# Softmax attention in phases of thirteen and twelve scores instead of sixteen

## The chip, the cores and the metric

The kernel runs on one core of a Trainium2 chip. The core has a matrix engine (TensorE, PE in the profile; PEld is its weight load), three engines for elementwise work (VectorE or DVE, ScalarE or ACT, GpSimd or POOL) and a queue that issues most of the DMA transfers (SP). TensorE writes to PSUM, a memory of eight banks of 512 float32 columns on 128 partitions. The metric is the device time of one execution in microseconds, the median of several.

## What is computed

Two blocks over the same 2048 tokens of 512 channels, mixed by a gate; all in float32.

```python
def _A_ref(x, wqkv, wo):
    H = 32; Dh = D // H                      # 32 heads of 16 channels
    q, k, v = qkv[0], qkv[1], qkv[2]
    scores = jnp.einsum("bhqd,bhkd->bhqk", q, k) * Dh ** -0.5
    p = _softmax(scores, axis=-1)
    o = jnp.einsum("bhqk,bhkd->bhqd", p, v)
    return o.transpose(0, 2, 1, 3).reshape(B, S, D) @ wo
def _B_ref(x, w1, b1, w2, b2):
    h = _layernorm(x, axis=-1)
    u = _gelu(jnp.einsum("bsd,sf->bdf", h, w1) + b1)      # F = 1792
    y = jnp.einsum("bdf,fs->bds", u, w2) + b2
    return y.transpose(0, 2, 1)
g = _sigmoid((x * gate_w).sum(-1, keepdims=True))
return g * _A_ref(x, A_wqkv, A_wo) + (1 - g) * _B_ref(x, ...)
```

The attention needs 32 x 2048 x 2048 exponentials, and only ScalarE computes them.

## The kernel before

The first 300 us project x to v, k and q and compute the first layer of block B. Then comes the attention, which fills the rest. The second layer of block B, and after it the output projection, are laid beside it on TensorE.

**Groups, scores and phases.** A group is two heads times half of the queries; there are 32 (`NG`). A *score* is one matmul of 128 keys by 512 queries for one head, into one PSUM bank, from a stack of K rows (`ks`) and one of Q rows (`qs`) that SP loads a group ahead (`load_q` at the group's first phase, `load_k` at its second; 8 and 6 DMAs). A group has 2 heads x 16 key blocks x 2 query blocks = 64 scores. They are worked off in four *phases* of sixteen (`PHASES, NSC = 4, 16`), 128 phases in all. The order of every engine's instructions in this part is the order of the code (`tc.manual_schedule`).

**One phase.** TensorE computes sixteen scores on half of its rows each; beside each of the first `n_b` of them, on the other half, runs a half of a matmul of the dense work (`dn`, up to 14 in a phase; a fence of a one-element memset on POOL, `token`, separates the two halves of the rows). The scores reach their exponentials in three ways. Four (`EVAC`) are copied out by DVE into `pe`, and ScalarE exponentiates the four in one instruction at the phase's end. Six (`SINGLE`) are read from PSUM one by one. Six form three doubles (`TWO`), each in two adjacent banks, exponentiated by one instruction of 1024 columns. Seven of the eight banks serve the scores; scores 7, 8 and 9 reuse banks of the first ones, and the doubles reuse banks of the others (`shares` gives which). After the scores follow the products with v: for each score two matmuls of 32 columns, added up in one bank (`av`), which DVE adds to the group's sum `ot`. The copied scores enter the products a phase later (`HELD`), and where it evens out, the last double too. After its last products a group's sum is stored by SP (`store`, eight DMAs), in the first phase of the next group, where the products run into two banks.

**Where the lines are.** L907 is the score matmul (tiles named `s`, or `t` for doubles), L916 the dense half beside it, L924 the copy by DVE, L928 a single exponential, L869 a double, L872 a double split into two singles (in a group's first phase, where one pair of banks must come free separately), L939 the block of four, L792 the products with v, L814 and L816 DVE's addition to the sum. L831 are dense matmuls that run before the loop. L492 fills constant rows of the K stacks. `later` holds work that DVE does after a phase's copies: splitting weights, inverting sums, and, at the change from second layer to output projection (`open_end`), constants for the end.

Of the kernel before, what the change touches and what calls it, by code (L numbers as in the profile page):

```python
# [16 lines left out]
SYNC = mybir.DependencyInfo(mybir.DependencyClass.Sync, mybir.DependencyReason.DATA)  # L17
REASON = "the two halves of the rows add to one bank"
# [40 lines left out]
def gated_mix(ctx: ExitStack, tc: tile.TileContext, a_x, a_wqkv, a_wo, b_w1, b_b1, b_w2, b_b2, gate_w, out):  # L59
# [438 lines left out]

    def stack(dst, src, which, pair, cols, planes):
        b, r0 = divmod(pair * 2 * DH, P)  # L500
        for i in range(2):
            rows = slice(r0 + i * DH, r0 + (i + 1) * DH)
            for row, *part in planes:
                at = slice(i * HALF + row, i * HALF + row + DH)
                nc.sync.dma_start(dst[at].bitcast(F32), src[b][part[which], rows, cols])
# [22 lines left out]
    PHASES, NSC, BANKS = 4, 16, 7  # L528
    LAST = NG * PHASES - 1
# [51 lines left out]
    def open_end():  # L581
# [6 lines left out]
        sums_of = end.tile([P, P], F32, name="sums_of")  # L588
        nc.vector.tensor_copy(
# [3 lines left out]
        least.append(end.tile([P, 1], F32, name="least"))  # L593
# [122 lines left out]
    for k in range(ND):  # L716
        call(6 * k + 5, load_wo, k, 6 * k + 5)
    steps = second_layer(0)
    first, at = steps[:28], put(steps[28:], 0, [14])
    for t in range(1, NS):  # L720
        at = put(second_layer(t), at, [14] * 3)
    for half in range(2):
        for k in range(ND):
            pairs = 3 if half and k == ND - 1 else 4
            p0 = PHASES * (half * NP + 4 * k + pairs) + 1
# [10 lines left out]
    p1 = PHASES * (NP + 2 * 4) + 3  # L736
    call(p1, fetch_o, 1, 0, (8, 9), (p1 + 2, p1 + 3, p1 + 3))
    call(p1 + 4, fetch_o, 1, 1, (10, 11), (p1 + 6, p1 + 7, p1 + 7))
    p2 = PHASES * (NP + 3 * 4) + 2
    assert p2 > 2 * at  # L740
    call(p2, fetch_o, 1, 2, (0, 1), (p2 + 1, p2 + 1, p2 + 1))
    call(p2 + 4, load_wq, p2 + 4)
    call(LAST - 1, fetch_o, 1, 3, (2, 3), (LAST, LAST, LAST), 3)
    for t in range(NH, NS):
        at = put_output(t, 6 if 2 * at < p2 + 2 else 8, at)
    assert at == NG * PHASES // 2
# [3 lines left out]
    EVAC = 1, 3, 5, 7  # L750
    SINGLE = 0, 2, 4, 6, 8, 9
    TWO = (10, 11), (12, 13), (14, 15)
    TURNS = [(0, 2), (4, 6), (8, 9), *TWO]
    HELD = [(1, 3), (5, 7)]

    def shares(n):

        for one in range(0, BANKS, 2):
            lows = [k for k in range(one)][::2] + [k for k in range(one + 1, BANKS)][::2]
            for third in lows:  # L760
                if n in (third, third + 1):
                    first, second = (low for low in lows if low != third)
                    return [first, first + 1, one, second, second + 1, 2 * third + 1 - n, n]

# [20 lines left out]
    def apply_v(av, grp, pairs, final=False):  # L785

        for n, pair in enumerate(pairs):
            for i, c, qb, pt in sorted(pair, key=lambda u: u[2]):
                for h in range(2):
                    j = 2 * qb + h  # L790
                    v_at = (c * H + grp % NP * 2 + i) * VC
                    nc.tensor.matmul(  # L792
                        av[32 * j : 32 * (j + 1), i * QC : (i + 1) * QC],
                        v_flat[:, v_at : v_at + 32],
                        pt[:, h * QC : (h + 1) * QC],
                        start=n == 0,
                        stop=n == len(pairs) - 1,
                    )
        covered = [{qb for pair in pairs for i, _, qb, _ in pair if i == n} for n in range(2)]
        assert all(len(c) != 1 for c in covered)  # L800
        if grp not in sums:
            sums[grp] = ot_pool.tile([P, NB], F32, name="ot"), [False, False]
        ot, begun = sums[grp]
        halves = [n for n in range(2) if covered[n]]
        if grp == NG - 1 and final:
            parts = [(x, y, True) for x, y in zip(column_halves(ot), column_halves(av))]
        elif len(halves) == 2 and begun[0] == begun[1]:
            parts = [(ot, av, begun[0])]
        else:
            cols = [slice(n * QC, (n + 1) * QC) for n in range(2)]  # L810
            parts = [(ot[:, cols[n]], av[:, cols[n]], begun[n]) for n in halves]
        for x, y, more in parts:
            if more:
                nc.vector.tensor_tensor(x, y, x, ALU.add)  # L814
            else:
                nc.vector.tensor_copy(x, y)  # L816
        for n in halves:
            begun[n] = True
        if final and grp < NG - 1:
            store(grp, sums.pop(grp)[0])  # L820

    engines = {getattr(mybir.EngineType, name) for name in ("PE", "Activation", "DVE", "Pool", "SP")}
    with tc.manual_schedule(engines=engines):
        kt, qt = {0: load_k(0)}, {0: load_q(0)}
        held, fence, turn, spare = [], None, 0, 0
# [9 lines left out]
        for p in range(LAST + 1):  # L835
            grp, ph = divmod(p, PHASES)
            second = ph % 2
            for what, *args in calls.get(p, ()):
                what(*args)
            if ph == 0:  # L840
                at = [[0, 0], [0, 0]]
                if grp + 1 < NG:
                    qt[grp + 1] = load_q(grp + 1)
            if ph == 1 and grp + 1 < NG:
                kt[grp + 1] = load_k(grp + 1)
# [3 lines left out]
            half = slice(0, HALF) if second else slice(HALF, P)  # L849

            head = [second if n < n_b else (n - n_b) % 2 for n in range(NSC)]
            qbs = {}
            for a, b in TURNS + HELD:
                if head[a] == head[b]:
                    qbs[a], qbs[b] = 0, 1
                else:
                    zero, one = (a, b) if head[a] == 0 else (b, a)
                    qbs[zero], qbs[one] = turn, 1 - turn
                    turn = 1 - turn

            swap = ph == PHASES - 1 and p < LAST and head[TWO[1][0]] == head[TWO[1][1]]
            order = [*TURNS[:4], TURNS[5], TURNS[4]] if swap else TURNS

            def exps(n):
                pt = ptp.tile([P, 2, NB], F32, name="p2", bufs=len(TWO) + 1)
                where = [share[(j - BANKS) % BANKS] for j in (n - 1, n)]
                low = min(where)
                if (low, low + 1) in twos:
                    nc.scalar.activation(pt, twos[low, low + 1], AF.Exp, scale=SCALE)  # L869
                else:  # L870
                    for m in range(2):
                        nc.scalar.activation(pt[:, m, :], twos[low + m], AF.Exp, scale=SCALE)  # L872
                for j, k in zip((n - 1, n), where):
                    units[j] = *units[j][:3], pt[:, k - low, :]

            evac = evp.tile([P, len(EVAC), NB], F32, name="pe")
            units = {}
            share = shares(spare)
            pool = regions()
            psum = pool.__enter__()  # L880
            ones = [psum.tile([P, NB], F32, name=f"s{n}") for n in range(BANKS)]
            for n in range(NSC):
                i, qb = head[n], qbs[n]
                c = at[i][qb]
                at[i][qb] += 1
                if n < TWO[0][0]:
                    if n >= BANKS:
                        ones[share[n - BANKS]] = psum.tile([P, NB], F32, name=f"s{share[n - BANKS]}")
                    s = ones[share[n % BANKS]]
                else:  # L890
                    if n == TWO[0][0]:
# [4 lines left out]
                        for low in range(BANKS):  # L896
                            if low == share[2]:
                                av = psum.tile([P, NB], F32, name="av")
                            elif low in share[3:5] and ph == 0:
                                twos[low] = psum.tile([P, NB], F32, name=f"s{low}")  # L900
                            elif low not in twos:
                                two = psum.tile([P, 2, NB], F32, name=f"t{low}")
                                twos[low], twos[low + 1] = two[:, 0, :], two[:, 1, :]
                                twos[low, low + 1] = two
                    s = twos[share[(n - BANKS) % BANKS]]
# [16 lines left out]
                if n in EVAC:  # L922
                    pt = evac[:, EVAC.index(n), :]
                    nc.vector.tensor_copy(pt, s)  # L924
                    units[n] = i, c, qb, pt
                elif n in SINGLE:
                    pt = ptp.tile([P, NB], F32, name="p1", bufs=len(SINGLE))
                    nc.scalar.activation(pt, s, AF.Exp, scale=SCALE)  # L928
                    units[n] = i, c, qb, pt
                else:  # L930
                    units[n] = i, c, qb, None
                    if n == TWO[0][1] or n == TWO[1][1] and not swap:
                        exps(n)
                    elif n == TWO[2][1]:
                        exps(n)
                        if swap:
                            exps(TWO[1][1])
# [202 lines left out]
```

## Time and profile before

| | us |
|---|---|
| median of 3 runs | 1293.9 (1292.6 to 1295.09) |
| the profiled execution | 1295.3 |
| its span in the trace | 1293.3 |
| attention: first score to the last phase's products | 304.7 to some 1272 |
| granted TensorE clock | 0.997 of full speed |

A row of the trace in order of time gives start, duration, engine, line, operation, output<-input, shape and the number of merged instructions; in a row of several, the duration reaches from the first start to the last end. The rows of stretches give, after the stretch and its length, busy time and instruction count of PE, PEld, DVE, ACT and POOL, then the clock, the DMA share and GB/s. Rows of the chain of waits give start, duration and what the chain ran through.

### The profile page before, as it was taken

The numbers are of one execution on the slowest core, as the hardware profiler recorded it, in microseconds if no ns is written. First come the engines' busy times: TensorE is split into PE (matmuls) and PEld (weight loads), VectorE is DVE, ScalarE is ACT, GpSimd is POOL, SyncE is SP. The second block draws the span as 40 slices with busy tenths as digits, with TensorE's granted clock in tenths as the row PEclk, the third lists the DMA queues.
The fourth block names the chain that finished last, engine by engine and source line by source line (L and its number), as shares of the span: only waits on it lengthen the run. The fifth ranks groups of instructions, "written<-read, shape, count | busy, mean of one in ns | idle before, by whom it ended". The sixth has DMA issues, their size and how long they took to land.

```text
span 1293.3 us, 33067 instructions
## 1 busy us (share of the span) xinstructions
PE 1280.4 (99%) x13278; PEld 850.4 (66%) x13278; DVE 671.0 (52%) x1155; ACT 1091.3 (84%) x1537; POOL 180.0 (14%) x272
## 2 busy tenths in 40 slices
PE   9999999999999999999999999999999999999997
PEld 7888888886666666666666666666665565655555
DVE  5675362438445545544544444454454665645555
ACT  3443343447999999999999999999999999999994
POOL 0210244553110111011011101101110000000000
PEclk9999999999999999999999999999999999999999
DMA  4497643327343343333334443333333654335411
GB/s 131 139 317 276 222 121 98 98 78 159 67 88 75 68 97 83 77 68 81 77 60 98 83 77 66 81 75 60 88 68 75 151 135 114 81 84 108 80 44 72
DMA packets 93581, 133.20 MB, mean 103 GB/s; under 512 B 16277, under 2 KB 55339, under 8 KB 90348
## 3 DMA queue, kind: packets, MB, share of 16 engines
q1 hardware_dynamic: 92844, 129.94, 41.2%
q8 instruction: 108, 1.77, 0.6%
q10 hardware_dynamic: 576, 1.05, 0.2%
q14 instruction: 53, 0.43, 0.1%
HBM read 97.00 MB, written 33.93 MB: 101 GB/s over the span
## 4 chain that ended last, share of the span: by engine, by line
PE 93%; ACT 4%; DVE 1%; issue 1%; DVEq 0%; ACTq 0%
PE av L792 28%; PE s L907 19%; PE acc L416 12%; PE t L907 10%; PE acc L73 10%; PE dn L916 6%; PE s L792 5%; ACT p L928 1%; ACT p L869 1%; ACT pe L939 1%; PE pa L996 1%; DVE pe L924 1%; PE acc L187 1%; PE dn L831 1%; PE acc L254 0%
## 5 line engine op out<-in xcount | busy, mean ns | idle before, releaser
L928 ACT ACTIVATE p<-s 128x512 f32<-128x512 f32 x768 | 395.7, 648 | 6.1 <-PE s L907 3.6
L869 ACT ACTIVATE p<-t 128x1024 f32<-128x1024 f32 x352 | 348.4, 1131 | 0.0
L907 PE MATMUL s<-qs,ks 64*128 64x512 f32 x1344 | 343.0, 404 | 1.1 <-DVE pe L924 0.7
L924 DVE COPY pe<-s 128x512 f32<-128x512 f32 x512 | 317.8, 683 | 6.9 <-PE s L907 6.4
L907 PEld LDWEIGHTS s<-qs,ks 64*128 64x128 f32 x1344 | 232.9, 184 | 97.5 <-issue 52.4
L792 PE MATMUL av<-p,v 128*32 128x256 f32 x4872 | 285.4, 379 | 0.0
L814 DVE TENSOR_TENSOR ot<-av,ot 128x512 f32<-128x512 f32 (+1 forms) x128 | 73.5, 575 | 396.6 <-PE av L792 396.6
L939 ACT ACTIVATE pe<-pe 128x2048 f32<-128x2048 f32 x129 | 259.5, 2014 | 0.0
L792 PEld LDWEIGHTS av<-p,v 128*32 128x32 f32 x4872 | 158.4, 110 | 104.9 <-issue 0.7
L907 PE MATMUL t<-qs,ks 64*128 64x512 f32 x704 | 185.1, 445 | 2.9 <-ACT p L928 0.4
L916 PE MATMUL dn<-u_lo,w_hi 64*128 64x512 f32 x430 | 174.1, 405 | 0.0
L916 PE MATMUL dn<-u_hi,w_lo 64*128 64x512 f32 x430 | 173.9, 404 | 0.0
L916 PE MATMUL dn<-u_hi,w_hi 64*128 64x512 f32 x428 | 173.2, 405 | 0.0
L66 POOL TENSOR_TENSOR w_lo<-w_raw,w_hi 128x512 fp32r<-128x512 f32 (+1 forms) x126 | 149.0, 1189 | 124.6 <-ACT w_hi L65 108.5
L907 PEld LDWEIGHTS t<-qs,ks 64*128 64x128 f32 x704 | 96.2, 184 | 83.4 <-ACT p L928 74.9
L792 PE MATMUL av<-pe,v 128*32 128x256 f32 x2048 | 138.1, 387 | 0.1
L920 POOL MEMSET token<- 1x1 f32 x124 | 12.7, 102 | 866.9 <-PE dn L916 811.2
L65 ACT CAST w_hi<-w_raw 128x512 fp32r<-128x512 f32 (+1 forms) x67 | 38.1, 569 | 79.2 <-PE acc L416 58.8
L792 PEld LDWEIGHTS av<-pe,v 128*32 128x32 f32 x2048 | 53.6, 109 | 54.2 <-ACT p L928 25.3
L416 PE MATMUL acc<-h_hi,w_hi 128*128 128x512 f32 x224 | 87.1, 389 | 0.0
L416 PE MATMUL acc<-h_lo,w_hi 128*128 128x512 f32 x224 | 87.1, 389 | 0.0
L416 PE MATMUL acc<-h_hi,w_lo 128*128 128x512 f32 x224 | 87.1, 389 | 0.0
(151 smaller groups left out, 1507.2 us busy)
## 6 DMA issues: line engine op xcount, KB each, us to landing
w_raw<-in_B_w_dram SPq DMA_DIRECT2D x96, 256.0 KB
ks<-kp SPq DMA_DIRECT2D x192, 128.0 KB
qs<-qp SPq DMA_DIRECT2D x256, 64.0 KB
qp<-pc SPq DMA_DIRECT2D x16, 768.0 KB
x<-in_A_x_dram SPq DMA_DIRECT2D x32, 256.0 KB
kp<-pc SPq DMA_DIRECT2D x16, 512.0 KB
w_raw<-in_B_w_dram SPq DMA_DIRECT2D x32, 128.0 KB
bp<-row SPq DMA_DIRECT2D x16, 256.0 KB
```

Source lines behind the costliest of these rows:

```text
L65: copy(hi, src)
L66: return sub(lo, src, hi.bitcast(F32), ALU.subtract)
L73: nc.tensor.matmul(ps, a, b, start=start and n == 0, stop=stop and n == last)
L416: nc.tensor.matmul(p, a, b, start=first and k == 0, stop=last and k == 2)
L792: nc.tensor.matmul(av[32 * j : 32 * (j + 1), i * QC : (i + 1) * QC], v_flat[:, v_at : v_at + 32], pt[:, h * QC : (h + 1) * QC], start=n == ...
L814: nc.vector.tensor_tensor(x, y, x, ALU.add)
L869: nc.scalar.activation(pt, twos[low, low + 1], AF.Exp, scale=SCALE)
L907: nc.tensor.matmul(s, kt[grp][rows_i, c * P : (c + 1) * P], qt[grp][rows_i, qb * NB : (qb + 1) * NB], start=True, stop=True,)
L916: mm = nc.tensor.matmul(ps, a[half], b[half], start=begin and not second, stop=last and bool(second))
L924: nc.vector.tensor_copy(pt, s)
L928: nc.scalar.activation(pt, s, AF.Exp, scale=SCALE)
L939: nc.scalar.activation(x, x, AF.Exp, scale=SCALE)
```

## The change

Two groups share ten phases of thirteen, thirteen, thirteen, thirteen, twelve, twelve, thirteen, thirteen, thirteen and thirteen scores (`SIZES`), 160 phases in all instead of 128. Phases five and six of each ten hold scores of both groups; the scores numbered in `SHARED` belong to the older. In a phase of thirteen DVE copies three scores (1, 3, 5), four are singles (0, 2, 4, 6) and six form doubles; in a phase of twelve it copies two. No bank is used three times in a phase any more. Which products run in which phase is planned ahead (`plan`): the newest group keeps back one or two of its last scores, so that each phase adds an even number. Products into two banks, and with them a double split in two singles, stand in three phases of ten instead of two of eight.

With it come these: the dense work is spread anew, 11, 11, 11 and 9 (or 10) beside the scores of a phase instead of 14, and 31 instead of 28 of its matmuls run before the loop; a group's sum is filled with zeros by POOL and then only added to; the products of every fourth and tenth phase wait, one each, for the fourteen loads of the next group's stacks (`await_loads`); the second K stack's constant rows are filled by POOL instead of DVE; the constants for the end are made eleven phases after `open_end` instead of at it; some loads of the output projection are issued in other phases.

```diff
-    PHASES, NSC, BANKS = 4, 16, 7
-    LAST = NG * PHASES - 1
+    SIZES, BANKS = (13, 13, 13, 13, 12, 12, 13, 13, 13, 13), 7
+    LAST = NP * len(SIZES) - 1
+    SHARED = 0, 2, 4, 5, 6, 7
...
-    first, at = steps[:28], put(steps[28:], 0, [14])
+    first, at = steps[:31], put(steps[31:], 0, [11])
...
+    on_dve(p0 + 11, end_constants)
...
-    EVAC = 1, 3, 5, 7
-    SINGLE = 0, 2, 4, 6, 8, 9
-    TWO = (10, 11), (12, 13), (14, 15)
+    EVAC = {13: (1, 3, 5), 12: (1, 3)}
+    SINGLE = {13: (0, 2, 4, 6), 12: (0, 2, 4, 5)}
+
+    def shares(n, size):
...
+                    a, b = (low for low in lows if low != third)
+                    other = 2 * third + 1 - n
+                    if size == 13:
+                        return [a, a + 1, b, other, b + 1, one, n], [a, b, third], one
+                    return [other, a, a + 1, b, b + 1, one], [third, a, b], one
...
+                if await_loads and n > 1 and landed:
+                    tc.add_manual_dep(mm.ins, landed.pop(0).ins.name, SYNC, reason=AHEAD_OF_USE)
...
+    def plan():
+        heads, owner, batches, sides = {}, {}, [], {}
+        waiting, turn = [], [0] * NG
+        for p in range(LAST + 1):
+            two, r = divmod(p, len(SIZES))
...
+            late = [(p, n) for n in EVAC[size]]
+            todo = waiting + [(p, n) for n in range(size) if n not in EVAC[size]]
...
+            newest = max(owner[u] for u in todo)
+            batches.append([])
+            waiting = []
+            for grp in sorted({owner[u] for u in todo}):
+                mine = [u for u in todo if owner[u] == grp]
+                if grp == newest and p < LAST:
+                    kept = 2 - len(mine) % 2
+                    mine, waiting = mine[:-kept], mine[-kept:]
+                batches[p].append((grp, mine))
...
+                    sums[grp] = ot_pool.tile([P, NB], F32, name="ot")
+                    nc.gpsimd.memset(sums[grp], 0.0)
...
             if p == 0:
-                shift_rows(nc.vector, k_bufs[1])
+                shift_rows(nc.gpsimd, k_bufs[1])
```

On TensorE, the turn from scores to products in a phase in the middle of the second layer, before (`t` is a double's pair of banks, `p` an exponentiated score or double, `pe` the block of copied scores of the phase before; the waits name the engine whose counter is awaited):

```order
L907 MATMUL t_7022<-qs,ks_2703 128x512 [waits DVE_49,Activation_49]
L907 MATMUL t_7022<-qs,ks_2703 128x512
L792 MATMUL av<-pe,v 32x256 [waits Activation_49]
L792 MATMUL av<-pe,v 32x256 x7
L792 MATMUL av<-p_6918,v 32x256 x4
L792 MATMUL av<-p_6979,v 32x256 x2
L792 MATMUL av<-p_6986,v 32x256 x2
L792 MATMUL av<-p_6993,v 32x256 x2
```

The same turn now, in a phase with the products of fourteen scores:

```order
L944 MATMUL t_7493<-qs,ks_2704 128x512 [waits DVE_49,Activation_49]
L944 MATMUL t_7493<-qs,ks_2704 128x512
L813 MATMUL av<-p_7416,v 32x256 [waits DVE_49]
L813 MATMUL av<-p_7416,v 32x256 x3
L813 MATMUL av<-pe,v 32x256 x6
L813 MATMUL av<-p_7465,v 32x256 x2
L813 MATMUL av<-p_7472,v 32x256 x2
L813 MATMUL av<-p_7479,v 32x256 x2
L813 MATMUL av<-p_7486,v 32x256 x2
L813 MATMUL av<-p_7498,v 32x256 [waits Activation_49]
L813 MATMUL av<-p_7498,v 32x256 x3
```

The last double still waits for DVE and ACT (now for the copy of score 3 and the single of score 6), the bank of the products for DVE's third copy instead of a single, and the copied scores are three, behind two that were kept.

On ACT, one phase before:

```order
L928 ACTIVATE p_10400<-s_10394 128x512
L928 ACTIVATE p_10407<-s_10393 128x512
L928 ACTIVATE p_10414<-s_10397 128x512
L928 ACTIVATE p_10421<-s_10391 128x512
L928 ACTIVATE p_10430<-s_10427 128x512
L928 ACTIVATE p_10435<-s_10432 128x512
L869 ACTIVATE p_10449<-t_10444 128x1024
L869 ACTIVATE p_10456<-t_10441 128x1024
L869 ACTIVATE p_10460<-t_10443 128x1024
L939 ACTIVATE pe<-pe 128x2048
```

and now:

```order
L965 ACTIVATE p_10424<-s_10418 128x512
L965 ACTIVATE p_10431<-s_10420 128x512
L965 ACTIVATE p_10438<-s_10421 128x512
L965 ACTIVATE p_10445<-s_10417 128x512
L971 ACTIVATE p_10457<-t_10453 128x1024
L971 ACTIVATE p_10463<-t_10454 128x1024
L971 ACTIVATE p_10469<-t_10452 128x1024
L978 ACTIVATE pe<-pe 128x1536
```

Two singles are gone, and the block at the end has three scores instead of four; the doubles stand as they did.

On TensorE, the products of a fourth phase now, where the loads of the next stacks are awaited (`DMAHW` are the counters of the DMA queues; before, the next group's first scores waited for them):

```order
L813 MATMUL av<-p_7607,v 32x256 x3
L813 MATMUL av<-pe,v 32x256 [waits DMAHW1_49]
L813 MATMUL av<-pe,v 32x256 [waits DMAHW2_49]
L813 MATMUL av<-pe,v 32x256 [waits DMAHW3_49]
L813 MATMUL av<-pe,v 32x256 [waits DMAHW4_49]
L813 MATMUL av<-pe,v 32x256 [waits DMAHW5_49]
L813 MATMUL av<-pe,v 32x256 [waits DMAHW6_49]
L813 MATMUL av<-p_7650,v 32x256 [waits DMAHW7_49]
```

and the first rows of a group's first phase before:

```order
L907 MATMUL s_7211<-qs,ks_2704 128x512 [waits DMAHW3_49,DMAHW2_49,DMAHW4_49,DMAHW1_49,DMAHW7_49,DMAHW0_49,PE_49]
L916 MATMUL dn<-u_lo,w_hi 128x512 [waits Pool_49]
L907 MATMUL s_7212<-qs,ks_2704 128x512
L916 MATMUL dn<-u_hi,w_lo 128x512
L907 MATMUL s_7210<-qs,ks_2704 128x512 [waits Activation_49]
```

Six of the waits of the first score, and those of a later one, moved into products of the phase before.

More of the change, by code (lines that the diff above doesn't have):

```diff
@@ L849, in gated_mix @@
             half = slice(0, HALF) if second else slice(HALF, P)
[L851 to L874, printed above, removed]
```

246 lines of the change are left out of this document (130 added, 116 removed).

## The prediction

> **What bounds the kernel now.** I read the page's sums and slices first, then the chain of waits, then busy time by stretch, then ScalarE's rows in order of time.
>
> ```profile
> span 1293.3 us, 33067 instructions
> PE 1280.4 (99%) x13278; PEld 850.4 (66%) x13278; DVE 671.0 (52%) x1155; ACT 1091.3 (84%) x1537; POOL 180.0 (14%) x272
> ACT  3443343447999999999999999999999999999994
> PE 93%; ACT 4%; DVE 1%; issue 1%; DVEq 0%; ACTq 0%
> ```
>
> The chain names TensorE for 93%, but it steps back along an engine as long as that engine looks busy, and TensorE's rows always overlap. The slices show ScalarE (ACT) full from the tenth slice on, which is the attention, and there it can be asked what is idle:
>
> ```profile
> 305.00:982.00 677.00, 676.48 (x8420) 426.00 (x8420) 330.12 (x589) 675.40 (x923) 75.48 (x149) 1.00 0.38 78
> 982.00:1272.00 290.00, 286.56 (x3400) 166.92 (x3396) 165.70 (x266) 286.75 (x391) 4.46 (x35) 0.99 0.43 95
> ```
>
> The fourth busy figure is ACT: 675.40 of 677.00 and 286.75 of 290.00 us. So the exponentials bound the attention, and any gain must come from their cost or from the little idle time. ACT rows overlap, so I price them by their ends, in a stretch where ACT runs without a pause:
>
> ```profile
> 1041.27 2.97 ACT L869 ACTIVATE p<-t 128x1024 f32<-128x1024 f32 x3
> 1043.98 2.04 ACT L939 ACTIVATE pe<-pe 128x2048 f32<-128x2048 f32 x1
> 1045.79 3.18 ACT L928 ACTIVATE p<-s 128x512 f32<-128x512 f32 x6
> 1048.65 3.06 ACT L869 ACTIVATE p<-t 128x1024 f32<-128x1024 f32 x3
> 1051.36 2.14 ACT L939 ACTIVATE pe<-pe 128x2048 f32<-128x2048 f32 x1
> ```
>
> Ends: 1044.24, 1046.02, 1048.97, 1051.71, 1053.50. Six singles take 2.95 (0.492 each), three doubles 2.74 (0.913), the block of four copied scores 1.79. A phase of sixteen is 7.48 us of ACT. One phase of before, seen from TensorE (PE), DVE and ACT:
>
> ```profile
> 711.88 0.50 PE L907 MATMUL s<-qs,ks 64*128 64x512 f32 x1
> 712.22 0.40 PE L907 MATMUL s<-qs,ks 64*128 64x512 f32 x1
> 712.46 0.39 PE L907 MATMUL s<-qs,ks 64*128 64x512 f32 x1
> ...
> 715.35 0.49 PE L907 MATMUL t<-qs,ks 64*128 64x512 f32 x2
> 715.78 0.42 PE L792 MATMUL av<-pe,v 128*32 128x256 f32 x4
> ```
>
> ```profile
> 712.72 2.48 DVE L924 COPY pe<-s 128x512 f32<-128x512 f32 x4
> ```
>
> ```profile
> 712.48 3.05 ACT L928 ACTIVATE p<-s 128x512 f32<-128x512 f32 x6
> 719.90 3.09 ACT L928 ACTIVATE p<-s 128x512 f32<-128x512 f32 x6
> ```
>
> The last two scores need the bank of the fourth DVE copy, which ends at 715.20; they start at 715.35, the products with v at 715.78 (0.43 later), and the next phase follows 3.59 us after (rows below), at 719.37. That is 7.49 us round PE and DVE, against 7.48 on ACT: two loops that tie.
>
> **The change, part by part.** *ACT's work.* Per extra 512 columns the rows give 0.421 (double less single) and 0.433 (four less one, by three); with 0.427 the block of three costs 1.79 - 0.427 = 1.363 and the block of two 0.936. A phase of thirteen is 4 x 0.492 + 2.74 + 1.363 = 6.07, one of twelve 5.643. A double split into two singles adds 0.984 - 0.913 = 0.07: 32 of them before (the 64 rows below), 47 after (three shared phases in each pair of groups but the first, which has two).
>
> ```profile
> L928 ACT ACTIVATE p<-s 128x512 f32<-128x512 f32 x768 | 395.7, 648 | 6.1 <-PE s L907 3.6 <-PE dn L916 1.1
> L869 ACT ACTIVATE p<-t 128x1024 f32<-128x1024 f32 x352 | 348.4, 1131 | 0.0
> L939 ACT ACTIVATE pe<-pe 128x2048 f32<-128x2048 f32 x127 | 257.2, 2025 | 0.0
> L872 ACT ACTIVATE p<-s 128x512 f32<-128x512 f32 x64 | 36.4, 655 | 0.0
> ```
>
> Before: 128 x 7.48 + 32 x 0.07 = 959.7. After: 128 x 6.07 + 32 x 5.643 + 47 x 0.07 = 960.9. **+1.2 us**; 0.01 of rounding in a phase is 1.4 us, so +0 to +3. Taking scores off ACT's singles pays nothing: every score still passes ACT, in as many instructions.
>
> *The loop round PE.* With three copies DVE drops out: at 0.62 a copy the third ends near 2.7 us after the phase's first score, and what waits for it (the bank of the products with v) comes later than 3. The third pair of scores, 11 and 12, now waits for the bank of the fourth single (score 6). In a stretch where ACT was behind, that sort of wait can be timed, and the length of the products by their number:
>
> ```profile
> 1048.53 0.50 PE L907 MATMUL t<-qs,ks 64*128 64x512 f32 x2
> ```
>
> ```profile
> 1049.02 1.07 PE L792 MATMUL av<-pe,v 128*32 128x256 f32 x16
> ```
>
> ```profile
> 715.85 3.59 PE av L792 x64
> 1071.96 3.16 PE av L792 x56
> 1086.80 4.02 PE av L792 x72
> ```
>
> The fifth of the six singles ended at 1048.97 - 0.49 = 1048.48, and the scores that waited for its bank started 0.05 later. A score is four rows of products: 14 scores 3.16, 16 scores 3.59, 18 scores 4.02, so 0.215 a score and 2.73 for 12. By the order the products now alternate: 12 scores in one phase, 14 in the next, since one or two scores of the last double are held back so that the number is even. From the end of the first single, then: three more singles 1.47; to the third pair 0.05; to the products 0.43; products; and from the next first score to its exponential's end 1.20 (712.48 + 3.05 - 5 x 0.49 = 713.08, less 711.88). That is 3.15 plus the products, of which I take 3.14 (the 0.43 reads 0.42 as often). With 12 scores 5.87, under ACT's 6.07: ACT is late and nothing is lost. With 14 scores 6.30: ACT waits **0.23 us**. What ACT was late by does not help, since the loop starts from ACT's own single. Of 64 phases with 14 (or, at the end, 18) scores, 57 have at most 11 dense matmuls beside them: 57 x 0.23 = 13.1. Seven, in the output projection with 12 beside 13 scores, begin products at 0.34 + 11 x 0.231 + 0.43 = 3.31 (the first step 711.88 to 712.22, then 0.231 each to the twelfth) and take 6.47: 0.40 each, 2.7 in all. **+15.8 us**. The bounds are 64 x 0.06 either way, 12 to 20, if each of the four pieces is off by 0.015.
>
> *Idle time that goes.* The two stretches hold 967.0 us, 7.3 above ACT's 959.7. Part of it has names:
>
> ```profile
> 298.13 6.63 PE dn L831 x28
> 309.37 1.76 DVE ks L492
> 311.60 1.76 DVE ks L492
> ...
> 1002.43 2.72 PE av L792 x24
> 1005.14 2.54 PE s L792 x40
> ```
>
> The constants of the end, in DVE's queue, made the products at 1002.43 take 5.26 instead of 3.59; they go eleven phases further on, behind that phase's copies; DVE is busy 166 of 290 us in that stretch. The fill of the second K buffer (two 1.76 us on DVE in the first phases) goes to POOL. The rest is small excess at group changes, and the start. I let two thirds go: **-4.8 us**, between -7.3 and -2. Three more matmuls ahead of the loop (31 instead of 28) cost 3 x 6.63/28 = **+0.7**, not hidden, since ACT has nothing to do before.
>
> *The waits put into the products.* Fourteen products in each fourth and tenth phase wait for one load of the next stacks each.
>
> ```profile
> L907 PEldq EVENT_SEMAPHORE  x508: 51/51/51, 303.2 to 1268.0; - x170
> ```
>
> ```profile
> 707.31 4.41 SPq L505 DMA_DIRECT2D ks<-kp  x6
> ```
>
> ```profile
> 715.50:724.00 8.50, 8.50 (x112) 5.20 (x116) 4.16 (x7) 8.50 (x13) 0.18 (x2) 1.00 0.01 3
> ```
>
> The phase began 7.49 before the one shown, at 704.39; the six loads of K were issued from 707.31, behind the stores of the group before, and by 715.50 the DMA queues are empty (share 0.01): 11.1 us after the phase's start. Now K is issued one phase into the pair and awaited two phases and half a phase on, some 16 us: landed. I cost the fourteen waits at 0, covered by products of 0.107 us each; queued behind them are the rest of the products and the next phase's scores, and above them the bound is 14 x 0.051 = 0.71 a group. The 32 fills of the sums on POOL come at a phase's start, six us ahead of DVE's add; POOL is busy 75 of 677 us: 0. Filling turns the first copy of a group into an add, the same 0.69.
>
> *Sum:* 1.2 + 15.8 - 4.8 + 0.7 = +12.9. The profiled execution took 1295.3 (span 1293.3 and 2.0 around it), 1.4 above the median 1293.9; the sum becomes 1308.2 for it and **1306.8** against the median.
>
> A row to weigh with a rule: the first score of a phase takes 0.34 to the second instead of 0.231, and from the last scores to the products pass 0.43. The Trainium skill (TensorEngine Tiling (Array Packing), Key Properties) says that changing the tiling mode, not just the tile, drains the engine; scores are 64-row tiles, products 32-column tiles, so it speaks against 32 more phases. The trace agrees, with 0.11 and 0.20 a switch.
>
> **The rivals.** (a) Only the switches count: the loop has slack, but 32 more phases pay (0.34 - 0.23) + (0.43 - 0.23) = 0.31 each on PE, 9.9 in place of 15.8: +7.0, 1301. For it: PE is 99% busy. Against: with both switches PE's own work in a phase of thirteen is 0.34 + 10 x 0.231 + 0.43 + 2.94 = 6.02 on average, under ACT's 6.07. (b) The other side: the 0.43 before the products is a wait of the old order (its sixth single ended at 715.53, 0.25 before the products) and not a cost. If it falls to 0.20 or less, 14 scores also fit into 6.07 and ACT never waits: 1.2 - 4.8 + 0.7 = -2.9, 1291. Against stands a phase in which scores and products came late:
>
> ```profile
> 489.54 0.59 PE L907 MATMUL t<-qs,ks 64*128 64x512 f32 x2
> 490.06 0.64 PE L792 MATMUL av<-pe,v 128*32 128x256 f32 x8
> ```
>
> ```profile
> 486.32 3.05 ACT L928 ACTIVATE p<-s 128x512 f32<-128x512 f32 x6
> ```
>
> The sixth single had ended at 489.37, 0.69 before, and the products still began 0.52 after the first of the scores. (c) It does not tell: a shorter 0.43 by half leaves 64 x 0.07, or 4.5: 1295.5. (d) The fourteen waits cost 0.051 each on PE's queue: both phases that hold them have 14 scores, so nothing hides them: 31 x 0.71 = 22 more, 1329. For it, such instructions show 51 ns; against, one wait fits into a matmul, as the products' waits for ACT do now.
>
> **How the numbers follow.** Forecast 0.66, (a) 0.10, (b) 0.08, (c) 0.09, (d) 0.07. The forecast's own range is 1302 to 1312. The range leaves out (b) and (d): 1295 to 1314. A measurement of this kernel tells 0.2%, 2.6 us. Faster is most of (b), 0.07; same is (c) and a rest, 0.11; slower 0.82.
>
> **What would show it.** Right: in the changed kernel ACT's rows still fill the attention, but each phase with 14 products shows ACT idle or its first single starting 0.59 after the phase's first score, and a period near 6.3, the neighbours with 12 near 5.9; the third pair starts right after the fourth single's end; DVE is waited for by nobody. The products at the phase of the constants keep their length. Wrong: periods of 12 and 14 together 12.14 or below, (b); gaps between products in each fourth phase, (d); ACT's block of three far from 1.36.

## The result, and the profile after

The changed kernel takes **1311.9 us** (median of four runs, 1310.45 to 1313.59) against 1294.1 for the kernel before, run beside it (1292.6 to 1295.1): a ratio of **1.0139, 95% interval 1.0122 to 1.0157**. It is 1.4% slower and 5.1 us more than forecast. The span of the profiled execution grew from 1293.3 to 1310.0, by 16.7 us.

The lines of the page that answer those shown of before, and busy time by stretch (PE, PEld, DVE, ACT, POOL; then the granted clock, the DMA share and GB/s), of the changed kernel:

```profile
span 1310.0 us, 33291 instructions
PE 1291.9 (99%) x13277; PEld 835.3 (64%) x13277; DVE 669.1 (51%) x1129; ACT 1096.8 (84%) x1552; POOL 200.8 (15%) x336
ACT  3444343448999999999999999999999999998994
PE 94%; ACT 2%; DMA 2%; DVE 1%; issue 1%; SPq 0%; DVEq 0%; ACTq 0%
```

```profile
305.00:1050.00 745.00, 742.71 (x9076) 445.66 (x9078) 352.68 (x604) 737.48 (x1012) 93.73 (x208) 1.00 0.37 74
1050.00:1295.00 245.00, 238.17 (x2791) 136.62 (x2784) 143.23 (x231) 231.60 (x318) 6.91 (x39) 0.99 0.44 102
```

Two things are new. In the chain of waits DMA has 2%, where before it had none worth naming; and the ACT slices have one 8 near the end. ACT is idle 7.5 us of the first stretch and 13.4 of the second (some 4 of these after its last exponential); before, it was nearly full in both.

**The steady loop.** Two phases in a row in the changed kernel on TensorE, the first with the products of 14 scores, the second with 12 (start, length, then what it is; L944 are scores, L813 products):

```profile
665.27 0.50 PE L944 MATMUL s<-qs,ks 64*128 64x512 f32 x1
...
667.69 0.49 PE L944 MATMUL t<-qs,ks 64*128 64x512 f32 x1
...
668.03 0.39 PE L944 MATMUL t<-qs,ks 64*128 64x512 f32 x1
...
668.26 0.42 PE L944 MATMUL t<-qs,ks 64*128 64x512 f32 x2
668.61 0.64 PE L813 MATMUL av<-p,v 128*32 128x256 f32 x8
...
671.77 0.50 PE L944 MATMUL s<-qs,ks 64*128 64x512 f32 x1
...
674.57 0.41 PE L944 MATMUL t<-qs,ks 64*128 64x512 f32 x2
674.91 0.41 PE L813 MATMUL av<-p,v 128*32 128x256 f32 x2
...
677.64 0.49 PE L944 MATMUL s<-qs,ks 64*128 64x512 f32 x1
```

The periods are 6.50 and 5.87, together 12.37. ACT over the same time:

```profile
664.63 1.54 ACT L978 ACTIVATE pe<-pe 128x1536 f32<-128x1536 f32 x1
666.01 2.12 ACT L965 ACTIVATE p<-s 128x512 f32<-128x512 f32 x4
667.92 2.96 ACT L971 ACTIVATE p<-t 128x1024 f32<-128x1024 f32 x3
670.63 1.62 ACT L978 ACTIVATE pe<-pe 128x1536 f32<-128x1536 f32 x1
672.37 2.07 ACT L965 ACTIVATE p<-s 128x512 f32<-128x512 f32 x4
```

The first block of copied scores ends at 666.17 and the four singles after it at 668.13: 1.96, or 4 x 0.49, nothing lost. The next block ends at 672.25 and its singles at 674.44: 2.19, so 0.23 is lost. Only 0.12 of that is a gap between rows (672.25 to 672.37). The rest hides inside the first single, which has no neighbour to overlap with. That is why busy time shows only half of what ACT loses, and why it has to be counted by the ends of rows. The loss stands at the start of the phase after the one with 14 products.

**One phase that the prediction did not see.** DVE where the third block of the layer's output is multiplied by its reciprocals (L988; L961 are the copies, L835 the addition of products to the sum), then what TensorE waited for, then the transfers in the chain of waits, all of the changed kernel:

```profile
1181.54 1.88 DVE L961 COPY pe<-s 128x512 f32<-128x512 f32 x3
1189.46 1.23 DVE L988 TENSOR_TENSOR o_sum<-e,o_sum 128x1024 f32<-128x1024 f32 x1 [6.04 <-DMA o_sum<-ri]
1190.72 0.69 DVE L988 CAST e<-o_sum 128x1024 fp32r<-128x1024 f32 x1
1191.34 0.68 DVE L835 TENSOR_TENSOR ot<-av,ot 128x512 f32<-128x512 f32 x1
```

```profile
1192.07 0.50 PE L944 MATMUL s<-qs,ks 64*128 64x512 f32 x2 [3.12 <-DVE ot L835]
```

```profile
1176.09 5.51 DMA ri<-inv
1181.62 7.75 DMA o_sum<-ri
```

DVE had inverted the sums by 1174.97. They go out to memory and come back broadcast, which lasts until 1189.37. DVE reached the multiply at 1183.42 and stood there for 6.04 us. Behind it in the same queue stood the addition that frees the bank of the products, which a score of the next phase needs. That phase, the 145th, takes 10.84 us (1187.29 to 1198.12); with the multiply later (first experiment) the same phase takes 5.44. Before, the same wait was there, but short:

```profile
1179.29 1.23 DVE L949 TENSOR_TENSOR o_sum<-e,o_sum 128x1024 f32<-128x1024 f32 x1 [1.81 <-DMA o_sum<-ri]
```

The multiply stands two phases of DVE's queue behind the inversion in both kernels, and the phases became shorter while the round trip did not: from the inverted sums to the landing it took 14.4 us now, and before some 13.7 (1165.62 to the multiply's start at 1179.29).

**Where the 16.7 us of span lie.** The first score comes 1.08 later (305.77 against 304.69), the attention lasts 985.5 instead of 969.1 (+16.3), the end is 0.7 shorter.

### The profile page after: what moved, and what is told of

The parts are those of the page before. It is cut to its first block, busy times and chain, and to the rows that moved or that the text cites. A ratio compares the mean times of both kernels' runs of the same rounds, so it can differ in the third digit from the quotient of the medians.

```text
span 1310.0 us, 33291 instructions
## 1 busy us (share of the span) xinstructions
PE 1291.9 (99%) x13277; PEld 835.3 (64%) x13277; DVE 669.1 (51%) x1129; ACT 1096.8 (84%) x1552; POOL 200.8 (15%) x336
## 4 chain that ended last, share of the span: by engine, by line
PE 94%; ACT 2%; DMA 2%; DVE 1%; issue 1%; SPq 0%; DVEq 0%; ACTq 0%
PE av L813 31%; PE s L944 20%; PE t L944 14%; PE acc L417 11%; PE acc L74 10%; PE s L813 4%; PE dn L953 3%; ACT p L965 1%; PE pa L1018 1%; DMA o_sum<-ri 1%; PE dn L890 1%; PE acc L188 1%; DMA ri<-inv 0%; PE acc L255 0%; DMA x<-in_A_x_dram 0%
## 5 line engine op out<-in xcount | busy, mean ns | idle before, releaser
L971 ACT ACTIVATE p<-t 128x1024 f32<-128x1024 f32 x433 | 429.4, 1132 | 0.4 <-PE t L944 0.4
L813 PE MATMUL av<-p,v 128*32 128x256 f32 x5536 | 384.1, 382 | 0.0
L965 ACT ACTIVATE p<-s 128x512 f32<-128x512 f32 x640 | 339.3, 660 | 14.3 <-PE s L944 4.9
L835 DVE TENSOR_TENSOR ot<-av,ot 128x512 f32<-128x512 f32 (+2 forms) x172 | 106.7, 621 | 435.6 <-PE av L813 435.1
L944 PE MATMUL s<-qs,ks 64*128 64x512 f32 x1182 | 313.2, 406 | 3.5 <-DVE ot L835 3.5
L961 DVE COPY pe<-s 128x512 f32<-128x512 f32 x448 | 282.5, 684 | 5.4 <-PE s L944 2.7
L944 PEld LDWEIGHTS s<-qs,ks 64*128 64x128 f32 x1182 | 202.3, 184 | 106.6 <-issue 60.4
L813 PEld LDWEIGHTS av<-p,v 128*32 128x32 f32 x5536 | 179.1, 110 | 141.3 <-issue 27.9
L978 ACT ACTIVATE pe<-pe 128x1536 f32<-128x1536 f32 (+1 forms) x161 | 242.4, 1507 | 0.0
L944 PE MATMUL t<-qs,ks 64*128 64x512 f32 x866 | 227.0, 432 | 5.6 <-DVE pe L961 1.5
L944 PEld LDWEIGHTS t<-qs,ks 64*128 64x128 f32 x866 | 110.8, 184 | 111.6 <-ACT p L965 97.8
L813 PE MATMUL av<-pe,v 128*32 128x256 f32 x1664 | 145.1, 383 | 0.0
L813 PEld LDWEIGHTS av<-pe,v 128*32 128x32 f32 x1664 | 61.8, 110 | 29.3 <-issue 0.5
```

Of the source, the lines that this page charges most:

```text
L813: mm = nc.tensor.matmul(av[32 * j : 32 * (j + 1), i * QC : (i + 1) * QC], v_flat[:, v_at : v_at + 32], pt[:, h * QC : (h + 1) * QC], start ...
L944: nc.tensor.matmul(s, kt[grp][rows_i, c * P : (c + 1) * P], qt[grp][rows_i, qb * NB : (qb + 1) * NB], start=True, stop=True,)
L971: nc.scalar.activation(pt, twos[k][2], AF.Exp, scale=SCALE)
L978: nc.scalar.activation(x, x, AF.Exp, scale=SCALE)
```

## The experiments

All times are medians in us, and each ratio is to the kernel before, run beside the experiment: 1293.7 for experiments 1 to 4, 1293.8 for 5 and 6, 1293.4 for 7.

**1. The multiply one phase later.** Nothing else is altered; the cast and the subtraction that follow it move too.

```diff
-    call(p2, fetch_o, 1, 2, (0, 1), (p2 + 1, p2 + 1, p2 + 2))
+    call(p2, fetch_o, 1, 2, (0, 1), (p2 + 2, p2 + 3, p2 + 3))
```

> The changed kernel with DVE's work on the third block of the output projection moved a phase later. Theory: the phase of 10.84 us in the changed kernel is DVE waiting 6.04 us for the inverted sums to land, with the copies of the next phase queued behind it; a phase later the wait is gone, 5 us less, about 1307. Rival: ACT makes the time up later, or the stall only moves to the next user of DVE: 1311 to 1312.

Measured: **1306.4** (1306.2 to 1306.9), ratio 1.0097 [1.0080, 1.0114], span 1304.7. DVE at that place:

```profile
1189.65 1.23 DVE L988 TENSOR_TENSOR o_sum<-e,o_sum 128x1024 f32<-128x1024 f32 x1 [0.35 <-DMA o_sum<-ri]
```

The first scores of the 145th and the 146th phase on TensorE:

```profile
1187.17 0.50 PE L944 MATMUL s<-qs,ks 64*128 64x512 f32 x1
...
1192.61 0.50 PE L944 MATMUL s<-qs,ks 64*128 64x512 f32 x1
```

The data lands as late as ever, but DVE now waits 0.35 for it. So 5.5 us of the loss are this one wait, and 12.7 remain for the loop and all else. The next experiments, but for the sixth, include this edit and are read against 1306.4.

**2. Twelve scores of products in every phase.** The first two scores' products are left out where there would be 14, so part of the sum over v is not computed. Scores, exponentials, copies, the number of phases and every change between scores and products stay.

```diff
-                apply_v(av, grp, [units.pop(u) for u in mine], final, await_loads=r in (3, 9) and n == len(batches[p]) - 1)
+                these = [units.pop(u) for u in mine]
+                these = these[2:] if len(these) == 14 else these
+                apply_v(av, grp, these, final, await_loads=r in (3, 9) and n == len(batches[p]) - 1)
```

> As the kernel with the later multiplication, and in each phase with the products of fourteen scores the first two scores' products are left out, so that every phase multiplies twelve (the sums lack them). Theory (a loop from ACT's fourth single over the third pair of scores and the products back to ACT is longer than ACT's work with fourteen, shorter with twelve): every phase of thirteen falls to ACT's 6.07, 6.09 in the output projection; 0.9 us for ten phases and 0.45 for seven others, 14 us less, about 1293. Rival 1, TensorE's own work bounds: 64 x 0.43 = 27 less, 1280. Rival 2, ACT's work bounds already: no change, 1307.

Measured: **1292.8** (1291.2 to 1295.2), ratio 0.9993 [0.9984, 1.0003]. Three first scores of phases on TensorE, and busy time (the fourth figure is ACT), of this kernel:

```profile
653.45 0.49 PE L944 MATMUL s<-qs,ks 64*128 64x512 f32 x1
...
659.37 0.50 PE L944 MATMUL s<-qs,ks 64*128 64x512 f32 x1
...
665.59 0.50 PE L944 MATMUL s<-qs,ks 64*128 64x512 f32 x1
```

```profile
305.00:1050.00 745.00, 741.71 (x8804) 444.05 (x8806) 358.04 (x612) 744.22 (x1028) 93.72 (x208) 1.00 0.38 77
```

5.92 + 6.22 = 12.14, which is twice the 6.07 that the prediction gave ACT for a phase of thirteen. ACT is busy 744.2 of 745.0. Ten phases of this kernel's steady loop take 60.06 (605.53 to 665.59), which is what the prediction's prices give for ACT's work in ten (8 x 6.07 + 2 x 5.643 + 3 x 0.07); the changed kernel takes 60.98 (366.62 to 427.60), or 0.23 more for each of the four phases with 14 products. So products are what ACT waits for, and without the surplus two scores the loop falls back to ACT's own time, neither less nor more. Rival (a) falls with it: the 32 additional phases with their mode switches are all still here, and what made the loss was the products. As TensorE has less to do in this experiment, it shows that the switches cost nothing where ACT sets the period, and not that they are free where TensorE is in the loop. The total also holds a wait that the changed kernel does not pay for: the 143rd phase takes 8.10 where its like take 5.93, since DVE stands there 2.90 for the sums that it is to invert (`inv<-r`).

**3. Four copies in a phase of thirteen.** DVE copies score 6 as well; ACT has three singles and a block of four, whose tile grows from three scores to four.

```diff
-    EVAC = {13: (1, 3, 5), 12: (1, 3)}
-    SINGLE = {13: (0, 2, 4, 6), 12: (0, 2, 4, 5)}
+    EVAC = {13: (1, 3, 5, 6), 12: (1, 3)}
+    SINGLE = {13: (0, 2, 4), 12: (0, 2, 4, 5)}
...
-            evac = evp.tile([P, 3, NB], F32, name="pe")
+            evac = evp.tile([P, 4, NB], F32, name="pe")
```

> As the kernel with the later multiplication, but in phases of thirteen DVE copies score 6 too, four copies and three singles. Theory: the third pair of scores waits for the fourth copy, which ends 3.32 after the phase's first score, so that products begin at 3.9 instead of 3.14 to 3.35 and phases last 6.63 and 7.06, 0.66 more on average: 128 x 0.66 = 84 more, about 1391. Rival, ACT's work decides: a block of four is cheaper than a single and a block of three by 0.06, 8 us less, 1299.

Measured: **1377.6**, ratio 1.0644 [1.0626, 1.0662]. DVE and TensorE in a phase of this kernel that begins at 687.88:

```profile
688.72 2.48 DVE L961 COPY pe<-s 128x512 f32<-128x512 f32 x4
```

```profile
691.25 0.50 PE L944 MATMUL t<-qs,ks 64*128 64x512 f32 x2 [0.44 <-DVE pe L961]
691.68 0.41 PE L813 MATMUL av<-p,v 128*32 128x256 f32 x2
```

The mechanism is as expected: the fourth copy ends at 691.20, the last pair starts 0.05 later, the products 0.43 after that, and the phases take 6.97 and 6.53. The size was too high by 13 us: in the steady loop a phase of thirteen lost 0.5 on average (ten phases take 64.98, 694.41 to 759.39, instead of 60.98) and not the 0.66 behind 1391. Over the whole attention it is 0.56 (71 us for 128 phases), in part because the 143rd phase takes 11.25, where DVE stands 3.18 for the sums that it is to invert. So a fourth copy puts DVE back into the loop at once, and three is what a phase of thirteen can hold.

**4. The loads of the next stacks not awaited in the products.** The waits go back to the next group's first scores.

```diff
-                apply_v(av, grp, [units.pop(u) for u in mine], final, await_loads=r in (3, 9) and n == len(batches[p]) - 1)
+                apply_v(av, grp, [units.pop(u) for u in mine], final, await_loads=False)
```

> As the kernel with the later multiplication, without the fourteen waits in the products of each fourth and tenth phase; the next group's scores wait for their stacks themselves. Theory: the waits in the products cost nothing (those phases last as long as their like), and before the scores they show as 0.1 to 0.2 us a group: 0 to 6 more, 1307 to 1313. Rival, each wait costs 0.051 on TensorE's queue: 22 less, 1285.

Measured: **1307.2** (1306.4 to 1307.6), against 1306.4 with the waits. They cost nothing that can be measured, and rival (d), 22 us, is out. The changed kernel's trace says the same: tenth phases (with the waits) take 6.50, eighth phases (without, also 14 scores) 6.51.

**5. The third pair no longer on the fourth single's bank.** If the loop is held by the wait of the third pair for the fourth single, an exchange of two banks should loosen it: score 6 goes where the products will be, and the third pair takes the banks of the second and third copy.

```diff
-                        return [a, a + 1, b, other, b + 1, one, n], [a, b, third], one
+                        return [a, a + 1, b, other, b + 1, n, one], [a, b, third], one
```

> The changed kernel with the later multiply of the experiment before (1306.4), and two scores of each phase of thirteen in swapped banks: the fourth single now lies in the bank that the products take, and the third pair takes the bank of the third DVE copy. Theory (the loop runs from the fourth single over the third pair to the products): the third pair then starts at 2.79 after the phase's first score also where ACT is late, and not at 3.00; a phase with 14 products takes about 6.30 instead of 6.50, so two phases take 12.17 against ACT's 12.14. About 4 phases of ten gain 0.2, where 12 dense matmuls do not fill the time: 9 us less, 1297 to 1299. Rival (the products and the mode switches fill TensorE by themselves, whatever the third pair waits for): 1306, unchanged. Rival (the fifth of the first seven scores now waits for the add that frees the bank of the products before, and DVE's copies shift): 1307 to 1315.

Measured: **1308.7** (two runs at 1305.3 and 1305.6, three at 1308.7 to 1309.6), ratio 1.0109 [1.0094, 1.0123]: no gain, and no change that can be told from 1306.4, as the first rival said. By the number alone the second rival (1307 to 1315) fits as well, but its mechanism is not in the trace: the third copy ends 2.73 after a phase's first score, as in the changed kernel (673.63 after 670.90 here, 674.50 after 671.77 there). The reason can be read in two phases with 14 products of this kernel. The first has eleven dense matmuls beside its scores:

```profile
666.85 0.50 PE L944 MATMUL t<-qs,ks 64*128 64x512 f32 x1
...
667.18 0.40 PE L944 MATMUL t<-qs,ks 64*128 64x512 f32 x1
...
667.42 0.39 PE L944 MATMUL t<-qs,ks 64*128 64x512 f32 x2
...
667.74 0.63 PE L813 MATMUL av<-p,v 128*32 128x256 f32 x7
```

The second pair starts at 666.85, when the third single has ended. From there TensorE runs by itself: 0.33, 0.24 and 0.32 to the products, since the dense matmuls keep the pair's scores one after the other. So the third pair does not wait at all, and the exchange does not touch what binds. The second phase has no dense matmuls (first scores of this phase, and of those before and after it):

```profile
1048.72 0.50 PE L944 MATMUL s<-qs,ks 64*128 64x512 f32 x2
...
1054.56 1.40 PE L944 MATMUL s<-qs,ks 64*128 64x512 f32 x7
...
1060.84 0.50 PE L944 MATMUL s<-qs,ks 64*128 64x512 f32 x2
```

The same three starts without the exchange (experiment 1):

```profile
1050.38 0.50 PE L944 MATMUL s<-qs,ks 64*128 64x512 f32 x2
...
1056.26 0.50 PE L944 MATMUL s<-qs,ks 64*128 64x512 f32 x2
...
1062.76 0.50 PE L944 MATMUL s<-qs,ks 64*128 64x512 f32 x2
```

5.84 + 6.28 = 12.12 with the exchange, 5.88 + 6.50 = 12.38 without. Here the pair's two scores run at once on the two halves of the rows, and the theory (6.30 and 5.87) holds to 0.03. So two chains of nearly equal length lead to the products: from the fourth single over the third pair, and from the third single over two pairs with dense matmuls beside them. Most phases have ten or eleven of those. With them the exchange only moves time from one phase to the next: the first scores at 664.49, 670.90 and 676.85 give 6.41 and 5.95, together 12.36, instead of 6.50 and 5.87. In the phase with 12 products, which begins at 670.90, the weight load of the third pair now waits for the third copy (its end is 673.63), and the products follow 0.42 behind the pair; in the changed kernel they follow after 0.34 (674.57 to 674.91):

```profile
671.74 1.89 DVE L961 COPY pe<-s 128x512 f32<-128x512 f32 x3
```

```profile
673.68 0.19 PEld L944 LDWEIGHTS t<-qs,ks 64*128 64x128 f32 x2 [0.26 <-DVE pe L961]
673.70 0.49 PE L944 MATMUL t<-qs,ks 64*128 64x512 f32 x2
674.12 0.41 PE L813 MATMUL av<-p,v 128*32 128x256 f32 x2
```

**6. The kernel before with the two side moves alone:** constants of the end later, fill of the second K buffer on POOL.

```diff
+    def end_constants():
...
+    on_dve(p0 + 9, end_constants)
...
-                shift_rows(nc.vector, k_bufs[1])
+                shift_rows(nc.gpsimd, k_bufs[1])
```

> The kernel before, with only the two side moves of the change: the constants of the end on DVE nine phases later (behind that phase's copies), and the fill of the second K buffer on POOL. Theory (this is the idle time that the prediction let go, 1.7 us for the constants and about 1 for the fill): 1291.0 to 1292.4 beside 1293.8 for the kernel before, so 1 to 3 us faster. Rival (DVE's and PE's loop of 7.49 has so little slack that the time comes back elsewhere): 1293 to 1294, no change.

Measured: **1292.7** (1292.0 to 1295.9), ratio 0.9989 [0.9980, 0.9999]: 1.2 us less by the medians, between 0.1 and 2.6, and the fastest kernel here, if by little. The median lies just above the expected range (up to 1292.4) and below the rival's (from 1293). Its profiled span, 1290.4, is 2.9 shorter, but the kernel before was profiled in an execution that was 1.4 above its median. The products that took 5.26 beside the constants, and the next phase's first score:

```profile
1000.62 1.07 PE L796 MATMUL av<-pe,v 128*32 128x256 f32 x16
...
1004.21 0.50 PE L911 MATMUL s<-qs,ks 64*128 64x512 f32 x2
```

They take 3.59 again. That phase is 2.26 shorter, the first two phases 0.9; 0.37 comes back where DVE meets the reciprocals' transfer, which lands no earlier.

**7. Both pairs on earlier banks.** The second pair takes the banks of scores 2 and 3, the third those of 4 and 5, the products that of 6.

```diff
-                        return [a, a + 1, b, other, b + 1, one, n], [a, b, third], one
+                        return [a, a + 1, b, b + 1, other, n, one], [a, b, third], one
```

> As the experiment with the swapped banks, and of the first seven scores the second pair's banks now hold the third and fourth (a single and a copy, free by 2.17 after the phase's first score), and the third pair's the fifth and sixth. Theory as the last run corrects it (the second pair waits for the third single, 2.22 or with a late ACT 2.43, and from there TensorE itself takes 0.34 + 0.23 + 0.34 to the products): the second pair now starts without a wait at about 2.20, the third when the third DVE copy ends, 2.77, and the products 0.42 after a pair that waited, at 3.19 in every phase of thirteen, ACT late or not. With 14 products a phase takes 6.35 and with 12 5.92; ten phases take 60.3 instead of 61.0, so 12 blocks of ten gain 8: 1297 to 1301. Rival (the prediction's step: only the third pair and the products matter, and those wait as in the last run): 1306 to 1309, no change.

Measured: **1310.3** (1310.2 to 1310.6), ratio 1.0133 [1.0116, 1.0149], slower than experiment 1 by 3.9. The corrected theory was not enough either. DVE's copies in a phase with 14 products that begins at 726.77, TensorE's weight loads for the pairs, the pairs, and from the rows of the scores' line the waits that are instructions of their own:

```profile
727.60 1.89 DVE L961 COPY pe<-s 128x512 f32<-128x512 f32 x3
```

```profile
729.00 0.18 PEld L944 LDWEIGHTS t<-qs,ks 64*128 64x128 f32 x1 [0.27 <-ACT p L965]
...
729.60 0.21 PEld L944 LDWEIGHTS t<-qs,ks 64*128 64x128 f32 x2 [0.27 <-ACT p L965]
```

```profile
729.63 0.49 PE L944 MATMUL t<-qs,ks 64*128 64x512 f32 x2
730.05 0.62 PE L813 MATMUL av<-p,v 128*32 128x256 f32 x5
```

```profile
L944 PEldq EVENT_SEMAPHORE  x452: 51/51/51, 301.9 to 1284.8; - x151
```

The third copy ends at 729.49, and the pair that needs it starts 0.14 later, where 0.05 was expected; the second pair likewise at 729.03, 2.26 after the phase's first score. Each pair's banks now come from ACT and from DVE, so each waits for two engines, and there are 452 waits as instructions of their own on the load queue, against 196 in experiment 5, whose pairs mostly wait for one engine. Products then start at 3.29 instead of 3.19, and the periods are 6.45 and 6.03, 12.48 together: ACT's lateness is indeed gone from the first, and the second pays for it.

## Why the prediction came out as it did

The side, the bound and the size of the loop's wait were right; one wait was missed. 1306.8 was forecast, and 1306.4 is what the kernel takes without that wait. That the two agree so closely is luck in part. Counted over the whole attention by the ends of ACT's rows (each row beyond its own time of 0.490, 0.917, 1.362 or 1.79), ACT is late in experiment 1 by some 17 us behind phases with 14 products and by some 1 elsewhere; in the kernel before it is late by some 8 in all. So the loop cost about 17 and not 15.8, the idle time that went was about 7 and not 4.8, and the two errors cancel but for 1 us.

- **ACT's work (+1.2): right.** By ends, in the steady loop, a single takes 0.490, a double 0.917, a block of three 1.362 (medians), against 0.492, 0.913 and 1.363 in the forecast. Experiment 2 gives 12.14 for two phases of thirteen and 60.06 for ten phases.
- **The loop (+15.8): the size was right, one step of it was not.** Two phases take 12.37 instead of ACT's 12.14: 0.23 for each phase with 14 products, as forecast. The step that failed is "The third pair of scores, 11 and 12, now waits for the bank of the fourth single (score 6)", 0.05 after its end, with 0.43 to the products. It holds where few dense matmuls or none stand beside the scores, as in the phase of experiment 1 that begins at 1056.26. In the phase shown of the changed kernel it is 0.13 (668.13 to 668.26) and 0.35, the same sum, because with eleven dense matmuls the third pair starts when TensorE gets to it, and what waited was the second pair, for the third single (667.69). The coincidence hid the error; experiment 5 brought it out. Where ACT's wait would show was also put wrongly: it shows in the phase after, and the phase with 14 has a period of 6.50 instead of "near 6.3", because ACT enters it late by the 0.20 by which the phase before is shorter than ACT's work (6.07 less 5.87).
- **Phases with twelve dense matmuls (0.40 each, which for seven is 2.8 and not 2.7):** 6.52 to 6.57 was measured instead of 6.47, and their neighbours with 12 scores take 6.10 and not 5.87, since the dense matmuls hold those too. Two phases lose 0.5.
- **Three more matmuls (+0.7): right.** The dense run before the loop starts 0.40 later in the changed kernel's profile (298.53 against 298.13), and the first score 1.08 later: 0.68 more.
- **Idle time that goes (-4.8): too small, and only the named part is tested.** Experiment 6 gives 1.2 by the medians and 2.9 by the spans for the two side moves, which its expectation put at 2.7. The count above gives about 7 for all of it; what took the rest away was not tested. With experiment 1's edit the attention is 11.1 longer than before (980.2 against 969.1), and the forecast for it was 12.2.
- **The fourteen waits (0): right**, by experiment 4.
- **What was missed: the multiply by the reciprocals.** The prediction asked whether K's loads land in time in shorter phases, and did not ask it of the other transfers that are counted in phases. The step that failed is the sum itself, which has no term for it: 5.5 us by experiment 1. Its sign "DVE is waited for by nobody" fails with it. The row with 1.81 in the kernel before was there to be seen, and from the phases' lengths the greater part of its growth to 6.04 follows: two phases of 5.87 and 6.50 are 2.6 shorter than two of 7.49.
- **The rivals.** (a) falls by experiment 2, (d) by experiment 4 and by the tenth phases. (b) and (c) need the step before the products to shrink: it did, from 0.43 to 0.35, but the start of the pair moved by as much the other way. The Trainium skill's rule that a change of tiling mode drains the engine (TensorEngine Tiling (Array Packing), Key Properties) agrees with the 0.34 from a phase's first score to its second. But the same 0.34 stands inside the scores behind a wait, where the mode does not change (667.69 to 668.03), so this step does not tell a change of mode from any other stop, and the 0.11 that the prediction counted for a switch is not shown to be one.

## What to carry to other kernels

When phases get shorter, list every wait whose distance is counted in phases and compare it with the transfer in microseconds: here a wait of 1.8 us grew to 6.0, and what stands behind it in the queue paid. Not each of them costs: of DVE's waits for the sums that it inverts, one went from 2.6 to 1.8 us and another from 1.4 to 3.6, and the phases around the second took 6.57 and 5.87, within 0.1 of their like. Where two engines tie, work out the time round the loop for each phase of the new rhythm and not for the mean: a load that alternates between 12 and 14 pays for the 14 and gets little back for the 12. And before a wait is taken away, look for the next chain that ends within 0.1 us of it; here there were three.

## What the runs showed of the hardware that was not expected

- What a wait for two engines costs depends on which of them comes last. A pair whose banks both come from DVE starts 0.05 to 0.06 after the copy it needs (experiments 3 and 5). Where ACT and DVE free one bank each and the copy is last, it is 0.14 (experiment 7) and 0.15 (the kernel before); there a 51 ns wait instruction for DVE stands ahead of the weight load, which waits for ACT itself. Where the single is last, as in a phase without dense matmuls of experiment 1, it is 0.06 again.
- Products follow a pair that had waited after 0.42 to 0.43, and a pair that ran straight on after 0.32 to 0.35. The forecast took 0.43 for both.
- The step from one score to the next is 0.33 to 0.34 behind any stop, whether TensorE came from products (665.27 and 671.77 in the changed kernel, 0.34 each) or had waited among the scores (667.69 to 668.03, 674.00 to 674.33), and 0.23 in a run without a stop.
- Two scores without dense matmuls beside them start together; with them they start 0.23 to 0.24 apart. That decides which of the two chains binds.
